# Attention pieces one tile later in the third to seventh chunk, and the second chunk's first weight splits behind an ELU operation

## The chip, the cores and the metric

The kernel runs on one core of a Trainium2 chip. The metric is device time in microseconds (us); the median of three runs of the kernel before is 904.67 us (904.6 to 905.83).

Five engines work side by side, each through its own queue in order: TensorE (PE; its weight loads are listed as PEld), VectorE (DVE), ScalarE (ACT), GpSimd (POOL) and SyncE (SP), which here only issues DMAs. They wait for each other by semaphores.

## What is computed

Attention over 8 batches of 8 heads, 576 positions of 64, then a feed-forward layer on its output, taken as 4608 tokens of 512:

```python
scores = q @ k.T / sqrt(64)           # heads 0-3: a window of 32; heads 4-7: every 4th position of 128
attn = softmax(where(mask, scores, -1e9))
x = (attn @ v).transpose(0, 2, 1, 3).reshape(4608, 512)
h = x @ w_in                          # 512 -> 2048
g = where(h > 0, h, exp(min(h, 0)) - 1)   # ELU
out = g @ w_out                       # 2048 -> 512
```

## The kernel before

**The feed-forward layer** goes by 9 chunks of 512 tokens (`c`, 0 to 8; NCH) and in each by 16 tiles of the 2048 hidden columns (`f`, 0 to 15; NF). For each tile `gemm1` multiplies the chunk's x by a tile of w_in into one PSUM bank `h`; `elu` (L386) makes g of it; `gemm2` (L409) multiplies g by a tile of w_out and adds it into four banks `o_ps`. From chunk 1 on every operand is split into a rounded part and the rest (`xh`, `xl` by `split_x`, L353; `gh`, `gl` by `elu`; the weights `wh`, `wl` by `split_w`, L132), and each product is three products, so that 12 matmuls of 128x512 make a `gemm1` and 12 a `gemm2`. `flush(LAG)` (L491) runs `gemm2` two tiles late: on TensorE the order is product of tile f, output group of tile f-2, product of f+1, output group of f-1. The last output group of a chunk therefore comes in tile 1 of the next one, and with it `store` (L417): four ACT copies `o<-o_ps` (L420), each with its DMA to `out`, through three buffers `o`.

**The ELU operation** is, in chunks 1 to 6: ACT copies h out of its bank (L390), ACT's exponential (L392), DVE's min and add (L401), DVE's max and add (L402), ACT's cast `gh` (L405), DVE's rest `gl` (L406). In those chunks there is a single bank for h, so the next product waits until L390 has copied it. In chunk 0 the banks alternate, ACT runs L392 and L394, and a DVE operation reads the bank and frees it (L397 up to tile 13, L399 for tiles 14 and 15); `hidden` lists these DVE operations, and `hidden[-3]` is that of tile 13.

**The attention** of batch c+1 is made in pieces between the tiles of chunk c. For chunks 1 to 6 the tuple `when` (L508) says behind which tiles they stand: first a scores piece for two head pairs, then their outputs piece, then the same for the other two. A *scores piece* (`scores_piece`, L311) is 144 small matmuls into three banks; after a third of them comes an ACT copy of a single column, `nothing` (L326), which orders the writes into the third bank, and the last third waits for it. DVE adds masks (L279), takes the maxima (L281), subtracts (L288), ACT exponentiates (L289), DVE sums, normalises (L290, L206 to L208) and transposes (L304), once for each head pair; SP loads the next q and k. An *outputs piece* (L336) is 48 matmuls, four ACT copies into `x32` (L194, L197), and loads of v.

**Order.** TensorE's instructions keep the order in which the program is written. On DVE and ACT a scheduler interleaves; `tc.issue_after(ins)` makes the instructions of its block that run on the engine of `ins` come behind it. In chunk 1 the loop at L521 splits the weights that chunk 0 left whole: for each pair an ACT cast and a DVE subtraction (L136, L137). The first two (`split < 2`) come behind the last transposes of batch 1 (`last_transpose[1]`), the others behind `split_x(1)`. A split takes the room of weights split before it, so that ACT's cast waits for an earlier DVE subtraction.

```python
when = () if c == 0 or c >= B - 1 else (0, 6, 7, 13) if c == 1 else (1, 6, 7, 12)
...
while c == 1 and split < min(NF, f + 2):
    left = [t for t in range(2) if wh[need[2 * split + t]] is None]

    with tc.issue_after(last_transpose[1] if split < 2 else last_x):
        if left:
            split_w(split, left[0], left[-1] + 1)
    split += 1
```

Of the kernel before, what the change touches and what calls it, by code (L numbers as in the profile page):

```python
# [18 lines left out]
B, H, S, D = 8, 8, 576, 64  # L19
# [27 lines left out]
def body(ctx: ExitStack, tc: tile.TileContext, q, k, v, masks, w_in, w_out, out):  # L47
# [37 lines left out]
    def load_w(k, behind=None):  # L85

        raw[k] = wst.tile([P, 2, DM], I64, name=f"r{k % NR}")
        if behind is not None:
            nc.gpsimd.tensor_copy(out=raw[k].bitcast(F32)[:QB, :, 0:1], in_=behind[:, 0:2].unsqueeze(2))
        for t in range(2):  # L90
            i = need[2 * k + t]
            nc.sync.dma_start(out=raw[k][:, t, :], in_=(w_in, w_out)[i % 2][i // 2])
# [6 lines left out]
    def magnitude(k):  # L99
        pair = full2[k] = wst.tile([P, 2, DM], F32, name=f"a{k}")  # L100
        for t in range(2):
            full[need[2 * k + t]] = pair[:, t, :]
        return nc.scalar.activation(out=pair.rearrange("p t c -> p (t c)"), in_=halves(k)[1].bitcast(F32), func=AF.Abs)

    def convert(k, keep=lambda ins: ins, part=slice(0, 2 * DM)):

        lo, hi = [u[:, part] for u in halves(k)]
        a = full2[k].rearrange("p t c -> p (t c)")[:, part]
        au = a.bitcast(U32)

        keep(nc.vector.tensor_scalar(out=a, in0=a, scalar1=TINY, scalar2=None, op0=ALU.max))  # L111

        keep(nc.vector.tensor_scalar(out=au, in0=au, scalar1=0x07FFFFFF, scalar2=3, op0=ALU.bitwise_and, op1=ALU.logical_shift_left))  # L113
        keep(nc.vector.scalar_tensor_tensor(out=au, in0=hi, scalar=0xC0000000, in1=au, op0=ALU.bitwise_and, op1=ALU.bitwise_or))  # L114

        return keep(nc.vector.scalar_tensor_tensor(out=au, in0=lo, scalar=29, in1=au, op0=ALU.logical_shift_right, op1=ALU.bitwise_or))  # L116
# [15 lines left out]
    def split_w(k, t0, t1):  # L132

        h, l = space(t1 - t0), space(t1 - t0)
        w = full2[k][:, t0:t1, :]
        nc.scalar.copy(out=h, in_=w)  # L136
        nc.vector.tensor_tensor(out=l, in0=w, in1=h.bitcast(F32), op=ALU.subtract)  # L137
        for t in range(t0, t1):
            wh[need[2 * k + t]], wl[need[2 * k + t]] = h[:, t - t0, :], l[:, t - t0, :]
        if all(wh[need[2 * k + t]] is not None for t in range(2)):  # L140
            spaces.append([f"a{k}", 2])
# [3 lines left out]
    last_transpose = [None] * B  # L145
# [190 lines left out]
    def outputs_piece(made):  # L336

        s = three()
        places = ((s[0], 0, 5), (s[1], 5, 6)), ((s[1][:, QB:], 0, 4), (s[2], 4, 6))
        for place, (b, hp, tr) in zip(places, made):  # L340
            products(place, v_of.pop(b * NPAIR + hp), tr)
        for place, (b, hp, _) in zip(places, made):
            if hp == 0:
                x32[b] = xp.tile([P, NPAIR, S], F32, name="x32", bufs=2)
            copies(b, hp, place)
        for b, hp, _ in made:
            load_v(b * NPAIR + hp + 2)
# [3 lines left out]
    hidden, below = [], []  # L351

    def split_x(c):  # L353
        for hp in range(NC):
            xh[hp] = xp.tile([P, TC], F32R, name=f"xh{hp}")
            xl[hp] = xp.tile([P, TC], F32R, name=f"xl{hp}")
            t0 = c * TC
            while t0 < (c + 1) * TC:
                b, o = divmod(t0, S)
                n = min(S - o, (c + 1) * TC - t0)  # L360
                u = slice(t0 - c * TC, t0 - c * TC + n)
                src = x32[b][:, hp, o:o + n]
                nc.scalar.copy(out=xh[hp][:, u], in_=src)
                last = nc.vector.tensor_tensor(out=xl[hp][:, u], in0=src, in1=xh[hp][:, u].bitcast(F32), op=ALU.subtract)
                t0 += n
        return last.ins
# [14 lines left out]
    def gemm1(c, f):  # L381
        for h_ps in first if (c, f) == (0, 0) else product1(c, f):
            pass
        return h_ps

    def elu(h_ps, c, f):  # L386
        e = fp.tile([P, TC], F32, name="e", bufs=3)
        if 0 < c < B - 1:
            h = fp.tile([P, TC], F32, name="h", bufs=2)
            nc.scalar.copy(out=h, in_=h_ps)  # L390
            h_ps = h
        nc.scalar.activation(out=e, in_=h_ps, func=AF.Exp)  # L392
        if c == 0:
            below.append(nc.scalar.activation(out=e, in_=e, func=AF.Relu, scale=-1.0, bias=1.0).ins)  # L394
            if f < F2:
                g = fp.tile([P, TC], F32, name="gh", bufs=3)
                hidden.append(nc.vector.scalar_tensor_tensor(out=g, in0=h_ps, scalar=0.0, in1=e, op0=ALU.max, op1=ALU.subtract).ins)  # L397
                return g, None
            hidden.append(nc.vector.scalar_tensor_tensor(out=e, in0=h_ps, scalar=0.0, in1=e, op0=ALU.max, op1=ALU.subtract).ins)  # L399
        else:  # L400
            nc.vector.tensor_scalar(out=e, in0=e, scalar1=1.0, scalar2=-1.0, op0=ALU.min, op1=ALU.add)  # L401
            nc.vector.scalar_tensor_tensor(out=e, in0=h_ps, scalar=0.0, in1=e, op0=ALU.max, op1=ALU.add)  # L402
        gh = fp.tile([P, TC], F32R, name="gh", bufs=3)
        gl = fp.tile([P, TC], F32R, name="gl", bufs=2)
        nc.scalar.copy(out=gh, in_=e)  # L405
        nc.vector.tensor_tensor(out=gl, in0=e, in1=gh.bitcast(F32), op=ALU.subtract)  # L406
        return gh, gl
# [79 lines left out]
    split = 0  # L487
# [3 lines left out]
    def flush(n):  # L491
        while len(pend) > n:
            c, f, g = pend.pop(0)
            if f == 0:
                o_of[c] = [ps_o.tile([P, DM], F32, name="o_ps") for _ in range(TC // P)]
            gemm2(o_of[c], g, f)
            if f == NF - 1:
                store(c, o_of.pop(c))

    att = second_attention()  # L500
    for c in range(NCH):
        if c == 1:
            with tc.issue_after(hidden[-4]), tc.issue_after(below[-4]):
                last_x = split_x(c)
        elif c > 1:
            split_x(c)

        when = () if c == 0 or c >= B - 1 else (0, 6, 7, 13) if c == 1 else (1, 6, 7, 12)  # L508
        for f in range(NF):
            while c == 0 and ready < min(NF, f + AHEAD):  # L510
                with tc.issue_after(below[-1] if below else last_copy.ins):
                    magnitude(ready)
                with tc.issue_after(last_conversion.ins):
                    last_conversion = convert(ready)
                if ready + NR < NF:
                    load_w(ready + NR)
                ready += 1
            if c == 0 and f == F1 - 3:
                with tc.issue_after(hidden[-1]), tc.issue_after(below[-1]):
                    split_x(0)  # L520
            while c == 1 and split < min(NF, f + 2):  # L521
                left = [t for t in range(2) if wh[need[2 * split + t]] is None]

                with tc.issue_after(last_transpose[1] if split < 2 else last_x):
                    if left:
                        split_w(split, left[0], left[-1] + 1)
                split += 1
            pend.append((c, f, elu(gemm1(c, f), c, f)))
            if c == 0 and F1 <= f + 2 <= NF:

                with tc.issue_after(hidden[-2]):
                    split_w(f + 1, 0, 2 if f >= F2 else 1)
            if c == 0:
                with tc.issue_after(hidden[-1] if f > 1 else last_step[NPAIR - 1]):
                    next(att)
            flush(LAG)
            if f in when:
                i = when.index(f)
                if i % 2 == 0:
                    made = scores_piece(c + 1, (i, i + 1))  # L540
                else:
                    outputs_piece(made)
# [60 lines left out]
```

## Time and profile before

| | us |
|---|---|
| median of three runs | 904.67 |
| the profiled execution | 905.6 |
| its span, first to last instruction | 903.7 |
| TensorE busy in the span | 883.6 |
| VectorE busy | 581.0 |
| ScalarE busy | 376.7 |

A row of the timeline holds the start in us from the span's start, the duration, engine, line and operation, the tiles (out<-in) and shapes, how many instructions are merged in it, and in brackets how long the engine sat idle before it and what ended that. A row of the windows view holds a stretch, its length, then the busy time of PE, PEld, DVE, ACT and POOL with the number of instructions, the granted TensorE clock, the DMA engines' share and GB/s. A row of the waits holds who waited for whom: us in total, times, longest. Nearly all matmuls have line 83, that of a helper; the tiles' names tell them apart.

### The profile page before, as it was taken

What the parts mean: (1) busy time and instruction counts of PE and PEld (TensorE: products, weight loads), DVE (VectorE), ACT (ScalarE), POOL (GpSimd) and SP (SyncE); (2) the same over time, 40 slices, a digit from 0 to 9 for tenths busy, and PEclk for the clock granted to TensorE, in tenths of its full rate; (3) what the DMA queues carried; (4) which work ended last, traced back from release to release, by engine and by line L of the source; (5) the groups of instructions that cost most, each with busy time, mean ns of one, the idle gap of its engine ahead of it and who ended that gap; (6) DMA issues with size and microseconds to landing.
All of it is one profiled execution on the core that took longest, in us unless ns stands there. A gap on an engine that the chain in (4) does not pass through costs nothing.

```text
span 903.7 us, 15468 instructions
## 1 busy us (share of the span) xinstructions
PE 883.6 (98%) x6540; PEld 695.3 (77%) x6540; DVE 581.0 (64%) x999; ACT 376.7 (42%) x750; POOL 6.0 (1%) x12
## 2 busy tenths in 40 slices
PE   6899999999999999999999999999999999999998
PEld 4544657788878887888788878888788888888886
DVE  5899999966485847694687559574859433343332
ACT  3755767434533343434443343434434432233222
POOL 2000000000000000000000000000000000000000
PEclk8999999999999999999999999999999999999999
DMA  9964103020122013111202111210210010001001
GB/s 341 406 228 145 45 19 100 19 90 1 43 94 89 2 36 102 36 55 36 102 7 84 36 48 54 90 34 2 102 37 1 1 47 1 1 0 47 1 1 46
DMA packets 23796, 59.35 MB, mean 66 GB/s; under 512 B 2640, under 2 KB 2736, under 8 KB 23728
## 3 DMA queue, kind: packets, MB, share of 16 engines
q1 hardware_dynamic: 23728, 58.37, 18.9%
q8 instruction: 51, 0.84, 0.4%
q14 instruction: 17, 0.14, 0.0%
HBM read 48.92 MB, written 9.44 MB: 65 GB/s over the span
## 4 chain that ended last, share of the span: by engine, by line
PE 82%; DVE 8%; DMA 5%; issue 2%; ACT 2%; SPq 0%; ACTq 0%; DVEq 0%
PE h L83 41%; PE o_ps L83 38%; PE a_ps L83 3%; DMA r<-w_out 2%; DVE a L116 1%; DVE a L114 1%; DMA out<-o 1%; DVE a L111 1%; DVE pt L304 1%; DMA r<-w_in 1%; DVE gh L397 1%; DVE r L137 1%; ACT o L420 1%; DVE a L113 1%; DMA kt<-k 1%
## 5 line engine op out<-in xcount | busy, mean ns | idle before, releaser
L83 PE MATMUL o_ps<-a,gh 128*128 128x512 f32 x816 | 267.8, 418 | 0.0
L83 PE MATMUL h<-xh,r 128*128 128x512 f32 x792 | 266.2, 394 | 0.5 <-DVE gh L397 0.5
L83 PEld LDWEIGHTS o_ps<-a,gh 128*128 128x128 f32 x816 | 152.8, 188 | 50.4 <-issue 22.0
L401 DVE TENSOR_SCALAR e<-e 128x512 f32<-128x512 f32 x128 | 54.6, 426 | 191.8 <-ACT e L392 189.9
L83 PEld LDWEIGHTS h<-xh,r 128*128 128x128 f32 x792 | 148.6, 188 | 35.6 <-DVE gh L397 2.1
L83 PE MATMUL h<-xl,r 128*128 128x512 f32 x412 | 160.6, 390 | 0.0
L405 ACT CAST gh<-e 128x512 fp32r<-128x512 f32 x130 | 80.9, 622 | 177.0 <-DVE e L402 176.7
L83 PE MATMUL o_ps<-a,gl 128*128 128x512 f32 x352 | 136.9, 389 | 0.0
L406 DVE TENSOR_TENSOR gl<-e,gh 128x512 fp32r<-128x512 f32 x130 | 89.6, 689 | 71.9 <-ACT gh L405 41.5
L392 ACT ACTIVATE e<-h 128x512 f32<-128x512 f32 x144 | 89.4, 621 | 103.6 <-PE h L83 100.9
L390 ACT COPY h<-h 128x512 f32<-128x512 f32 x96 | 56.2, 585 | 117.7 <-PE h L83 117.6
L304 DVE STREAM_TRANSPOSE pt<-sm 32x384 f32<-32x384 f32 x168 | 95.4, 568 | 2.2
L83 PE MATMUL o_ps<-r,gh 128*128 128x512 f32 x304 | 96.2, 389 | 0.0
L402 DVE SCALAR_TENSOR_TENSOR e<-h,e 128x512 f32<-128x512 f32 x128 | 88.2, 689 | 3.5
L83 PEld LDWEIGHTS h<-xl,r 128*128 128x128 f32 x412 | 77.3, 188 | 17.0 <-issue 1.2
L83 PE MATMUL h<-xh,a 128*128 128x512 f32 x256 | 85.5, 395 | 0.0
L83 PEld LDWEIGHTS o_ps<-a,gl 128*128 128x128 f32 x352 | 66.1, 188 | 13.8
L83 PEld LDWEIGHTS o_ps<-r,gh 128*128 128x128 f32 x304 | 57.1, 188 | 11.8
L83 PE MATMUL o_ps<-r,gl 128*128 128x512 f32 x168 | 65.5, 390 | 0.3 <-DVE gl L406 0.3
L83 PEld LDWEIGHTS h<-xh,a 128*128 128x128 f32 x256 | 48.0, 188 | 11.0
L83 PE MATMUL h<-xl,a 128*128 128x512 f32 x128 | 50.0, 391 | 0.0
L289 ACT ACTIVATE sm<-sm 96x768 f32<-96x768 f32 x24 | 20.4, 849 | 45.0 <-DVE sm L288 45.0
(100 smaller groups left out, 751.4 us busy)
## 6 DMA issues: line engine op xcount, KB each, us to landing
vt<-v SPq DMA_DIRECT2D x30, 384.0 KB, 3.6
kt<-k SPq DMA_DIRECT2D x30, 304.0 KB, 4.6
qt<-q SPq DMA_DIRECT2D x30, 288.0 KB, 3.8
r<-w_in SPq DMA_DIRECT2D x16, 512.0 KB, 8.0
r<-w_out SPq DMA_DIRECT2D x16, 512.0 KB, 8.2
out<-o SPq DMA_DIRECT2D x32, 256.0 KB, 2.8
out<-xl SPq DMA_DIRECT2D x4, 256.0 KB, 2.1
r<-v SPq DMA_DIRECT2D x2, 384.0 KB, 8.3
```

The lines of the kernel that those rows point to most:

```text
L83: return inorder(nc.tensor.matmul(*args, **kw))
L111: keep(nc.vector.tensor_scalar(out=a, in0=a, scalar1=TINY, scalar2=None, op0=ALU.max))
L113: keep(nc.vector.tensor_scalar(out=au, in0=au, scalar1=0x07FFFFFF, scalar2=3, op0=ALU.bitwise_and, op1=ALU.logical_shift_left))
L114: keep(nc.vector.scalar_tensor_tensor(out=au, in0=hi, scalar=0xC0000000, in1=au, op0=ALU.bitwise_and, op1=ALU.bitwise_or))
L289: nc.scalar.activation(out=sm, in_=sm, func=AF.Exp, scale=0.125)
L304: last_transpose[b] = nc.vector.transpose(out=tr[ks, :, cs], in_=sm[cs, :, rs]).ins
L390: nc.scalar.copy(out=h, in_=h_ps)
L392: nc.scalar.activation(out=e, in_=h_ps, func=AF.Exp)
L401: nc.vector.tensor_scalar(out=e, in0=e, scalar1=1.0, scalar2=-1.0, op0=ALU.min, op1=ALU.add)
L402: nc.vector.scalar_tensor_tensor(out=e, in0=h_ps, scalar=0.0, in1=e, op0=ALU.max, op1=ALU.add)
L405: nc.scalar.copy(out=gh, in_=e)
L406: nc.vector.tensor_tensor(out=gl, in0=e, in1=gh.bitcast(F32), op=ALU.subtract)
```

## The change

Two lines change:

```diff
-        when = () if c == 0 or c >= B - 1 else (0, 6, 7, 13) if c == 1 else (1, 6, 7, 12)
+        when = () if c == 0 or c >= B - 1 else (0, 6, 7, 13) if c == 1 else (2, 7, 8, 13)
...
-                with tc.issue_after(last_transpose[1] if split < 2 else last_x):
+                with tc.issue_after(last_transpose[1] if split < 2 else last_x), tc.issue_after(hidden[-3]):
```

In chunks 2 to 6 the four pieces stand behind tiles 2, 7, 8 and 13 in place of 1, 6, 7 and 12. In chunk 1 the weight splits must also stand behind the DVE operation (L397) of chunk 0's tile 13.

The first lines on ACT, at tile 1 of chunk 2, before (h_2363 is the scores piece's third bank, h_2483 the bank of tile 2's product):

```order
L420 COPY o<-o_ps 128x512 x3
L405 CAST gh<-e 128x512
L420 COPY o<-o_ps 128x512
L326 COPY nothing<-h_2363 96x1
L289 ACTIVATE sm<-sm 96x768
L390 COPY h<-h_2483 128x512
L392 ACTIVATE e<-h 128x512
L405 CAST gh<-e 128x512
```

And now (h_2361 is the bank of tile 2's product, h_2402 the piece's third bank):

```order
L420 COPY o<-o_ps 128x512 x3
L405 CAST gh<-e 128x512
L420 COPY o<-o_ps 128x512
L390 COPY h<-h_2361 128x512
L392 ACTIVATE e<-h 128x512
L405 CAST gh<-e 128x512
L326 COPY nothing<-h_2402 96x1
L289 ACTIVATE sm<-sm 96x768
```

The copy `nothing` and the exponential L289 moved from behind the last output copy to behind the ELU operation of tile 2. The same holds in chunks 3 to 6. On DVE the piece's first mask addition (L279) now follows the gl (L406) of tile 2 where it followed that of tile 1.

On DVE at the end of chunk 0 (r_1223, r_1315 and r_1318 are rests of split weights, h_1177 is the bank of tile 13, h_1202 that of tile 14):

```order
 L304 STREAM_TRANSPOSE pt_79<-sm 32x12x32 x6
+L397 SCALAR_TENSOR_TENSOR gh<-h_1177,e 128x512
+L137 TENSOR_TENSOR r_1223<-a_1132,r_1195 128x1024
 L137 TENSOR_TENSOR r_1315<-a_326,r_1223 128x1024
 L137 TENSOR_TENSOR r_1318<-a_474,r_1315 128x1024
-L397 SCALAR_TENSOR_TENSOR gh<-h_1177,e 128x512
-L137 TENSOR_TENSOR r_1223<-a_1132,r_1195 128x1024
 L399 SCALAR_TENSOR_TENSOR e<-h_1202,e 128x512
```

L397 of tile 13 and the split r_1223 moved ahead of the two splits r_1315 and r_1318; the four stand between the same neighbours as before.

On ACT at the same place (the a tiles are weights cast into the room of others, x_539 is batch 1's attention output):

```order
 L392 ACTIVATE e<-h_1202 128x512
+L136 CAST a_1570<-a_540 128x1024
 L194 COPY x_539<-a_ps_1226 128x288
 L394 ACTIVATE e<-e 128x512
+L194 COPY x_539<-a_ps_1227 128x288
 L136 CAST a_1609<-a_616 128x1024
-L194 COPY x_539<-a_ps_1227 128x288
-L136 CAST a_1570<-a_540 128x1024
 L405 CAST gh<-e 128x512
```

The cast a_1570, which takes the room of the weights that r_1223 reads, now stands ahead of tile 14's L394 and of the two copies. The order of SP's DMAs and of POOL's instructions is the same.

## The prediction

> **What bounds the kernel now.** Chunks are counted from 0 (c), their tiles from 0 (f); "the change's chunks" are c = 2 to 6. I read the page's table of busy times first, then two stretches of the windows view.
>
> ```profile
> span 903.7 us, 15468 instructions
> ...
> PE 883.6 (98%) x6540; PEld 695.3 (77%) x6540; DVE 581.0 (64%) x999; ACT 376.7 (42%) x750; POOL 6.0 (1%) x12
> ```
> ```profile
> 225.00:250.00 25.00, 24.30 (x224) 19.98 (x218) 10.90 (x22) 12.95 (x28) 0.00 (x0) 1.00 0.18 61
> 725.00:750.00 25.00, 25.00 (x112) 20.70 (x111) 7.97 (x14) 7.65 (x13) 0.00 (x0) 1.00 0.12 43
> ```
> TensorE is the bound: from 725 to 750, where no piece of attention runs, it is busy all 25.00 us at a granted clock of 1.00 while VectorE (DVE) and ScalarE (ACT) are busy under a third of the time. So the span shrinks only by time in which TensorE waits. From 225 to 250, inside the change's chunks, 0.70 us of it are missing. The view of waits says for what:
>
> ```profile
> PEld h L83 <- ACT nothing L326: 5.4, 5, 1.1
> ...
> PE h L83 <- ACT nothing L326: 4.6, 5, 0.9
> ```
> Five times, once for each of the change's chunks, TensorE waits for the tiny copy `nothing` in the middle of a scores piece. The timeline shows the piece behind tile 1 of chunk 2 (first three rows: its first matmul, the wait, the next tile's first matmul) and the piece behind tile 7 of the same chunk (first matmul, next tile's first matmul):
>
> ```profile
> 248.08 0.24 PE L83 MATMUL h<-kt,qt 64*32 64x64 f32 x1
> ...
> 250.23 0.24 PE L83 MATMUL h<-kt,qt 64*32 64x64 f32 x1 [0.93 <-ACT nothing L326]
> ...
> 250.87 0.50 PE L83 MATMUL h<-xh,r 128*128 128x512 f32 x1
> ...
> 286.13 0.24 PE L83 MATMUL h<-kt,qt 64*32 64x64 f32 x1
> ...
> 287.75 0.50 PE L83 MATMUL h<-xh,a 128*128 128x512 f32 x1
> ```
> The same 144 matmuls take 250.87 - 248.08 = 2.79 us behind tile 1 and 287.75 - 286.13 = 1.62 us behind tile 7. ACT's timeline gives the cause, first around tile 1, then around tile 7:
>
> ```profile
> 246.63 1.54 ACT L420 COPY o<-o_ps 128x512 f32<-128x512 f32 x3
> 248.05 0.64 ACT L405 CAST gh<-e 128x512 fp32r<-128x512 f32 x1
> 249.54 0.59 ACT L420 COPY o<-o_ps 128x512 f32<-128x512 f32 x1 [0.85 <-DMA out<-o]
> 250.02 0.16 ACT L326 COPY nothing<-h 96x1 f32<-96x1 f32 x1
> ...
> 285.99 0.62 ACT L405 CAST gh<-e 128x512 fp32r<-128x512 f32 x1 [1.22 <-DVE e L402]
> 286.87 0.16 ACT L326 COPY nothing<-h 96x1 f32<-96x1 f32 x1 [0.26 <-PE h L83]
> 290.40 0.85 ACT L289 ACTIVATE sm<-sm 96x768 f32<-96x768 f32 x1 [3.37 <-DVE sm L288]
> 291.15 0.57 ACT L390 COPY h<-h 128x512 f32<-128x512 f32 x1
> ```
> Tile 1 is where the previous chunk's four output copies stand. The fourth waits 0.85 us for the DMA that frees its buffer, and `nothing` stands behind it, so it starts 1.94 us into the piece. Behind tile 7 it starts 0.74 us in, after 0.26 us of waiting for TensorE itself, and TensorE does not wait.
>
> **Part one: the pieces of chunks 2 to 6 go one tile later.** Nothing is added or removed: the same 20 pieces (4 in each of 5 chunks) between tiles of the same kind, and the same order on the DMA queue. I go through each.
>
> *First scores piece, tile 1 to 2.* Behind the output copies now come tile 2's h copy, exponential and gh cast, and only then `nothing`: the same row order as at tile 7. I take tile 7's price, 1.62 us, for all five: 5 x (2.79 - 1.62) = 5.85 us gained. The lower bound of this gain by a row is the bare idle time, 4.6 us; the rest, 0.24 us a time, is matmuls that start slowly after the wait, and it goes with the wait.
>
> The Trainium skill, page "Perfetto Trace Analysis", section "Identifying the Most-Contended Engine", holds that matmul busy time misleads on TensorE and that the busy share of weight loads is the measure. By it the gain would be the weight loads' wait in the row above, 5.4 us; the trace here lies past both, since it times the whole piece.
>
> *What the wait covered.* With the piece gone from there, tile 2's product comes straight after the output group and the first tile of the new output group writes the banks that the four copies empty. Chunk 7 has no pieces and is that case already. Its fourth copy, and TensorE's next output group:
>
> ```profile
> 732.13 0.59 ACT L420 COPY o<-o_ps 128x512 f32<-128x512 f32 x1 [0.49 <-DMA out<-o]
> ...
> 733.93 0.39 PE L83 MATMUL o_ps<-r,gh 128*128 128x512 f32 x1
> ```
> The copy is done at 732.72, 1.21 us before the group begins, and the 725 to 750 window has no idle time. In chunk 2 the copy ends at 249.54 + 0.59 = 250.13. How long an output group (and a product) takes is in the chain of waits, and when tile 8's gl is made, behind the piece at tile 7, on VectorE's timeline:
>
> ```profile
> 253.92 2.72 PE o_ps L83 x12
> ```
> ```profile
> 294.35 0.68 DVE L406 TENSOR_TENSOR gl<-e,gh 128x512 fp32r<-128x512 f32 x1
> ```
> Tile 2's product would start where the piece does now, at 248.08, and the group 2.72 later, at 250.80: 0.67 us to spare, and the bank in question is the group's last. I cost it at nothing; were that slack gone, each microsecond would be paid in full. The scheduler also moves VectorE's rows; in chunk 2 alone the piece's six transposes now stand between two ELU operations of tile 3. At tile 7 the next tile's gl is done 295.03 - 286.13 = 8.9 us after the piece starts; 3.48 us of transposes (row further down) make it 12.4, and it is asked for after the piece and five groups, 1.62 + 5 x 2.72 = 15.2. No cost.
>
> *Outputs pieces, 6 to 7 and 12 to 13, and second scores piece, 7 to 8.* Each stays five tiles behind its scores. Chunk 1 has its last outputs piece behind tile 13 before the change. Its last copy:
>
> ```profile
> 226.39 0.34 ACT L194 COPY x<-h 128x192 f32<-128x192 f32 x1
> ```
> All that follows, the split for chunk 2 too, lies in the 225 to 250 window, whose missing 0.70 us are the stall's own (250.23 - 0.93 = 249.30, to 250). So tile 13 costs nothing. The loads that SyncE issues after each piece start a tile later and have five tiles left.
>
> **Part two: weight splits behind the ELU operation of tile 13.** Chunk 0's end, in TensorE's rows (an output group, the wait behind it, a later group of the same kind and its end), VectorE's and ACT's:
>
> ```profile
> 128.88 3.70 PE L83 MATMUL o_ps<-a,gh 128*128 128x512 f32 x8
> 133.08 0.50 PE L83 MATMUL h<-xh,r 128*128 128x512 f32 x1 [0.50 <-DVE gh L397]
> ...
> 137.21 3.70 PE L83 MATMUL o_ps<-a,gh 128*128 128x512 f32 x8
> 140.34 0.79 PE L83 MATMUL h<-xh,r 128*128 128x512 f32 x1
> ```
> ```profile
> 126.57 3.48 DVE L304 STREAM_TRANSPOSE pt<-sm 32x384 f32<-32x384 f32 x6
> 130.06 2.36 DVE L137 TENSOR_TENSOR r<-a,r 128x1024 fp32r<-128x1024 f32 x2
> 132.34 0.69 DVE L397 SCALAR_TENSOR_TENSOR gh<-h,e 128x512 f32<-128x512 f32 x1
> 132.94 1.22 DVE L137 TENSOR_TENSOR r<-a,r 128x1024 fp32r<-128x1024 f32 x1
> 134.07 0.69 DVE L399 SCALAR_TENSOR_TENSOR e<-h,e 128x512 f32<-128x512 f32 x1
> ```
> ```profile
> 134.19 1.05 ACT L136 CAST a<-a 128x1024 fp32r<-128x1024 f32 x1 [0.39 <-DVE r L137]
> 135.15 0.62 ACT L405 CAST gh<-e 128x512 fp32r<-128x512 f32 x1
> ```
> The two splits of 2.36 us stood ahead of L397, which frees a bank of h. It moves from 132.34 to 130.06, when TensorE needs no bank yet, and the wait goes: the group takes 4.20 us (133.08 - 128.88) where its like takes 3.13, so TensorE is 1.07 us early at 133. But VectorE has the same four operations to do: L399 still starts at 134.07, and the cast of 134.19 is only exchanged for another that waits for a split ending at the same time. So gh is cast at 135.15 as before. From there the second chunk's start is paced by VectorE:
>
> ```profile
> 140.00:168.00 28.00, 28.00 (x257) 22.09 (x255) 27.80 (x46) 16.24 (x28) 0.00 (x0) 1.00 0.24 82
> ```
> ```profile
> 167.56 0.69 DVE L406 TENSOR_TENSOR gl<-e,gh 128x512 fp32r<-128x512 f32 x1
> ```
> ```profile
> 168.30 0.50 PE L83 MATMUL o_ps<-r,gl 128*128 128x512 f32 x1 [0.30 <-DVE gl L406]
> ```
> It is busy 27.80 of 28.00 us, and at 168.30 TensorE waits for its gl. That moment doesn't come earlier, so the 1.07 us are spent waiting before it. I take 0. Ends: 1.07 us gained if VectorE could be early after all; 1.05 us lost if the cast that now stands ahead of tile 14's L394 on ACT (its like is the 1.05 us row) holds L399 up by its whole length.
>
> **Sum.** Profiled execution: span 903.7 - 5.85 = 897.9; with the 1.9 us outside its span (905.6 - 903.7) 899.7. Its time lies 0.9 above the runs' median, so against the median: 904.67 - 5.85 = 898.8 us.
>
> **Rivals.**
> *A, both parts pay.* VectorE's run up to 168 has a gap that the early bank fills: 904.67 - 5.85 - 1.07 = 897.8. For: the wait at 133 is real. Against: 27.80 of 28.00. Chance 0.10.
> *B, part of the stall comes back.* `nothing` now stands behind tile 2's gh, which hangs on VectorE. At tile 7 the cast ends at 286.61, 0.26 us before TensorE's results are there, and TensorE wants the bank some 0.2 us after the copy (estimate: two thirds of 1.62 after 286.13 is 287.21, the copy ends 287.03). If gh is 0.5 to 1 us later than that at tile 2, each stall keeps 0.3 to 0.8 us, with the slow restart: 1.5 to 4 us of the gain go, 900.3 to 902.8. Against: before tile 2's ELU VectorE has only ELU work, as before tile 7. Chance 0.10.
> *C, nothing changes.* The wait only changes its name, because `nothing` still stands behind something 1.9 us late: 904.7. The fourth output copy would have to end some 2 us later than 250.13: 0.67 us to tile 2's h copy, the 0.4 us of B, and the 0.93 us of the wait. Chance 0.04.
> *D, slower.* Behind `nothing` on ACT stands the piece's exponential (L289), which holds the next tile's h copy (L390) while it waits for VectorE, and the next product needs that one bank. At tile 7 the copy ends at 291.72; the next product but one starts here:
>
> ```profile
> 293.34 0.39 PE L83 MATMUL h<-xh,r 128*128 128x512 f32 x1
> ```
> So there are 1.6 us to spare, and beyond that TensorE stops. If the six transposes of another piece (3.48 us) came to lie ahead of the subtraction that L289 waits for, each piece would lose 3.48 - 1.6 + 0.24 = 2.1 us, five times 10.6, less 5.85: 909.4. It decides from 1.6 + 0.93 = 2.5 us of delay. Against: the order has the masks' additions right behind tile 2's gl, with no transposes between. Chance 0.04.
>
> **Numbers.** The forecast has 0.72, A 0.10, B 0.10, C 0.04, D 0.04. About 0.2%, 1.8 us, is what a measurement of this kernel can tell from no change, so faster means under 902.9: forecast, A and B, 0.92; same is C, 0.04; slower is D, 0.04. The range runs from A with a little scatter (runs of before lie between 904.6 and 905.83) to the nearer part of B and part two's loss with scatter: 897.3 to 901.2.
>
> **What would show it.** In the profile of the changed kernel: the waits for `nothing` gone from TensorE's list; the scores piece behind tile 2 taking 1.62 us; chunk 2 starting (its first product) at the same time as before within 0.3 us; L397 of tile 13 starting near 130.1, no wait at 133, but a wait for `nothing` or gl between 145 and 168 in its place. Wrong would be: a new wait of TensorE for h copies or output banks at tiles 2 to 4 of chunks 2 to 6, or a chunk 2 that starts 0.5 us or more earlier or later.

## The result, and the profile after

The changed kernel takes 899.28 us (median of 4 runs, 898.99 to 900.04) beside 904.86 us for the kernel before (4 runs, 904.6 to 905.83): a ratio of 0.9937, 95% interval 0.9921 to 0.9952. That is 5.58 us less; 898.8 us was forecast. The profiled execution took 900.04 us with a span of 898.2 us, 5.5 us less than the span before.

In the profile excerpts below, rows between those shown are left out. The page's first table in the changed kernel, then ScalarE's (ACT) waits for the output DMAs and both ways of waiting around `nothing`, two rows of the kernel before and three of the changed one:

```profile
span 898.2 us, 15468 instructions
PE 882.7 (98%) x6540; PEld 695.4 (77%) x6540; DVE 581.0 (65%) x999; ACT 376.3 (42%) x750; POOL 6.0 (1%) x12
```
```profile
ACT o L420 <- DMA out<-o: 5.2, 7, 0.9
ACT nothing L326 <- PE h L83: 1.8, 7, 0.3
```
```profile
ACT o L420 <- DMA out<-o: 4.2, 7, 0.7
ACT nothing L326 <- PE h L83: 2.9, 11, 0.3
PE h L83 <- ACT nothing L326: 0.2, 1, 0.2
```

Before, TensorE waited five times for `nothing` and ACT seven times the other way; now ACT's copy is the one that waits, 11 times of 12. The output copies still wait for their DMA seven times, 4.2 us in all in place of 5.2: most of that wait is still there, but in chunks 2 to 6 TensorE no longer waits for anything behind it. The scores piece behind tile 2 of chunk 2, in the rows that answer to those around tile 1 before (ACT's queue, then TensorE's first matmul of the piece, of its last third and of the next tile):

```profile
249.63 0.59 ACT L420 COPY o<-o_ps 128x512 f32<-128x512 f32 x1 [0.65 <-DMA out<-o]
253.67 0.62 ACT L405 CAST gh<-e 128x512 fp32r<-128x512 f32 x1 [1.22 <-DVE e L402]
254.55 0.15 ACT L326 COPY nothing<-h 96x1 f32<-96x1 f32 x1 [0.26 <-PE h L83]
```
```profile
253.81 0.24 PE L83 MATMUL h<-kt,qt 64*32 64x64 f32 x1
254.78 0.22 PE L83 MATMUL h<-kt,qt 64*32 64x64 f32 x1
255.43 0.50 PE L83 MATMUL h<-xh,r 128*128 128x512 f32 x1
```

`nothing` starts 254.55 - 253.81 = 0.74 us into the piece, after 0.26 us of waiting for TensorE, to the hundredth as behind tile 7 before, and the piece takes 255.43 - 253.81 = 1.62 us. The last third's first matmul starts 0.97 us into the piece and 0.65 us ahead of the product; before, behind the wait, it started 250.23 - 248.08 = 2.15 us in and 250.87 - 250.23 = 0.64 us ahead. So the matmuls behind the wait lost nothing. The 0.24 us by which the stall exceeded its listed 0.93 us lie ahead of the restart: idle time is counted from the end of the last matmul's row, and these rows, 0.22 to 0.24 us long each and 144 of them in 1.62 us, overlap. Two of the stretches in which the kernel before lost time:

```profile
225.00:250.00 25.00, 25.00 (x140) 20.85 (x137) 10.73 (x21) 12.84 (x28) 0.00 (x0) 1.00 0.17 57
250.00:275.00 25.00, 25.00 (x248) 20.61 (x247) 20.23 (x37) 9.18 (x17) 0.00 (x0) 1.00 0.20 67
```

No idle time is left in them. At the seam of chunks 0 and 1, TensorE (the first two matmuls of tile 15's product, the start of chunk 1's scores piece and of its last third, the next product, the output group of tile 2), VectorE (DVE), and the windows view:

```profile
132.26 0.79 PE L83 MATMUL h<-xh,r 128*128 128x512 f32 x1
132.89 0.39 PE L83 MATMUL h<-xl,r 128*128 128x512 f32 x1
145.77 0.24 PE L83 MATMUL h<-kt,qt 64*32 64x64 f32 x1
147.18 0.24 PE L83 MATMUL h<-kt,qt 64*32 64x64 f32 x1 [0.18 <-ACT nothing L326]
147.81 0.50 PE L83 MATMUL h<-xh,r 128*128 128x512 f32 x1
168.54 0.50 PE L83 MATMUL o_ps<-r,gl 128*128 128x512 f32 x1 [0.31 <-DVE gl L406]
```
```profile
126.80 3.48 DVE L304 STREAM_TRANSPOSE pt<-sm 32x384 f32<-32x384 f32 x6
130.31 0.69 DVE L397 SCALAR_TENSOR_TENSOR gh<-h,e 128x512 f32<-128x512 f32 x1
130.91 3.49 DVE L137 TENSOR_TENSOR r<-a,r 128x1024 fp32r<-128x1024 f32 x3
134.32 0.68 DVE L399 SCALAR_TENSOR_TENSOR e<-h,e 128x512 f32<-128x512 f32 x1
```
```profile
140.00:168.00 28.00, 27.79 (x255) 21.82 (x253) 27.80 (x46) 15.91 (x29) 0.00 (x0) 1.00 0.24 82
```

The wait at 133 is gone and tile 15's product starts at 132.26. But this execution runs 0.24 us behind the other by then (transposes at 126.80 against 126.57), and so does L399 (134.32 against 134.07): VectorE's four operations fill the same time in the new order. At 147.18 TensorE now waits for `nothing`, which it did not before, and at 168.54 for gl, again 0.24 us behind. The early bank was given back in between. Four rows of the kernel before (the second matmul of tile 15's product, the start of the piece, the product behind it, tile 3's product), then in the changed kernel the weight loads (PEld) that waited and ScalarE's rows ahead of them:

```profile
133.42 0.40 PE L83 MATMUL h<-xl,r 128*128 128x512 f32 x1
146.32 0.24 PE L83 MATMUL h<-kt,qt 64*32 64x64 f32 x1
147.94 0.50 PE L83 MATMUL h<-xh,r 128*128 128x512 f32 x1
159.09 0.50 PE L83 MATMUL h<-xh,r 128*128 128x512 f32 x1
```
```profile
158.32 0.30 PEld L83 LDWEIGHTS o_ps<-r,gh 128*128 128x128 f32 x2 [0.42 <-ACT o L420]
159.32 0.19 PEld L83 LDWEIGHTS h<-xh,r 128*128 128x128 f32 x1 [0.47 <-ACT h L390]
```
```profile
146.02 1.05 ACT L136 CAST a<-a 128x1024 fp32r<-128x1024 f32 x1 [0.67 <-DVE a L137]
146.98 0.14 ACT L326 COPY nothing<-h 96x1 f32<-96x1 f32 x1
153.42 0.62 ACT L136 CAST a<-a 128x512 fp32r<-128x512 f32 x1 [0.35 <-DVE a L137]
158.68 0.59 ACT L390 COPY h<-h 128x512 f32<-128x512 f32 x1
```

Counted from the output group ahead of tile 15's product (128.88 before, 129.12 after), the piece starts 17.44 us later in the kernel before and 16.65 us later in the changed one: 0.79 us early. It then takes 147.81 - 145.77 = 2.04 us in place of 1.62, which leaves 0.37 us, and tile 3's product starts 30.20 us after the group where it started 30.21: nothing is left. So the early time was gone at 159, ahead of the wait for gl at 168. The first part went to `nothing`, which stood behind a cast that had waited 0.67 us for VectorE: the same kind of stall as behind the output copies. The second went to ScalarE's last output copy and tile 2's h copy, at the end of a stretch in which ScalarE has no gap (153.42 to 159.27) and which begins with another cast that waited for VectorE.

To set this apart from the start, I measure each profile between three matmuls: the output group ahead of chunk 0's tile 15 product, the first product of chunk 2, and the first product of chunk 7. Before, then after:

```profile
128.88 0.70 PE L83 MATMUL o_ps<-a,gh 128*128 128x512 f32 x1
237.11 0.39 PE L83 MATMUL h<-xh,r 128*128 128x512 f32 x1
720.33 0.39 PE L83 MATMUL h<-xh,r 128*128 128x512 f32 x1
```
```profile
129.12 0.70 PE L83 MATMUL o_ps<-a,gh 128*128 128x512 f32 x1
237.40 0.39 PE L83 MATMUL h<-xh,r 128*128 128x512 f32 x1
714.76 0.39 PE L83 MATMUL h<-xh,r 128*128 128x512 f32 x1
```

"Seam" below is the first stretch, 108.23 us before and 108.28 after; "middle" is the second, chunks 2 to 6, 483.22 us before and 477.36 after, 5.86 us less.

### The profile page after: what moved, and what is told of

Read it like the earlier page. It is cut to its first block, busy times and chain, and to the rows that moved or that the text cites. A ratio compares the mean times of both kernels' runs of the same rounds, so it can differ in the third digit from the quotient of the medians.

```text
span 898.2 us, 15468 instructions
## 1 busy us (share of the span) xinstructions
PE 882.7 (98%) x6540; PEld 695.4 (77%) x6540; DVE 581.0 (65%) x999; ACT 376.3 (42%) x750; POOL 6.0 (1%) x12
## 4 chain that ended last, share of the span: by engine, by line
PE 84%; DVE 10%; ACT 2%; issue 2%; DMA 1%; POOL 0%; SPq 0%; DVEq 0%; ACTq 0%
PE h L83 41%; PE o_ps L83 39%; PE a_ps L83 4%; DVE a L116 1%; DVE a L114 1%; DVE r L137 1%; DVE a L111 1%; DVE pt L304 1%; DVE gh L397 1%; DVE a L113 1%; ACT pt L263 1%; DMA kt<-k 1%; DVE sm L208 1%; DMA r<-w_out 0%; ACT sm L269 0%
## 5 line engine op out<-in xcount | busy, mean ns | idle before, releaser
L406 DVE TENSOR_TENSOR gl<-e,gh 128x512 fp32r<-128x512 f32 x130 | 89.5, 689 | 71.8 <-ACT gh L405 42.2
L289 ACT ACTIVATE sm<-sm 96x768 f32<-96x768 f32 x24 | 20.3, 848 | 47.7 <-DVE sm L288 47.7
```

The source lines that it names most:

```text
L289: nc.scalar.activation(out=sm, in_=sm, func=AF.Exp, scale=0.125)
```

## The experiments

The theory is that of the prediction: the gain is five waits for `nothing` behind the output copies, and the early bank is lost to VectorE's backlog. All kernels were timed beside the kernel before; seam and middle are read from the same three matmuls of each profile.

| kernel | us | ratio to before, 95% | seam | middle |
|---|---|---|---|---|
| before | | 1 | 108.23 | 483.22 |
| the change | 899.28 | 0.9937 (0.9921 to 0.9952) | 108.28 | 477.36 |
| pieces alone | 899.33 | 0.9938 (0.9925 to 0.995) | 108.19 | 477.36 |
| splits alone | 905.17 | 1.0 (0.9991 to 1.0009) | 108.23 | 483.29 |
| first piece alone | 899.75 | 0.9943 (0.993 to 0.9955) | 108.24 | 477.39 |
| fourth output elsewhere | 900.2 | 0.9946 (0.9933 to 0.996) | 108.26 | 478.50 |
| one tile earlier | 899.27 | 0.9937 (0.9924 to 0.995) | 108.20 | 477.37 |
| chunk 1 later | 898.01 | 0.9926 (0.9912 to 0.994) | 107.36 | 477.30 |
| chunk 1 later, with the splits | 897.44 | 0.9918 (0.9905 to 0.9931) | 106.57 | 477.29 |

The kernel before took 905.04 us beside the first four experiments and 904.8 beside the last three.

**The two parts, each alone.**

```diff
-        when = () if c == 0 or c >= B - 1 else (0, 6, 7, 13) if c == 1 else (1, 6, 7, 12)
+        when = () if c == 0 or c >= B - 1 else (0, 6, 7, 13) if c == 1 else (2, 7, 8, 13)
```

> Part one alone: the four pieces of chunks 2 to 6 behind tiles 2, 7, 8, 13; the weight splits of chunk 1 as before. Theory (the whole gain is the five waits for `nothing` behind the output copies, 5 x 1.17 us): 5.6 to 5.9 us under the kernel before, as the full change; the stretch from the output group ahead of chunk 0's tile 15 product to chunk 2's first product takes 108.2 us as before. Rival (the splits give about 1 us and the pieces only the bare idle time): 4.6 us under, the stretch unchanged.

```diff
-                with tc.issue_after(last_transpose[1] if split < 2 else last_x):
+                with tc.issue_after(last_transpose[1] if split < 2 else last_x), tc.issue_after(hidden[-3]):
```

> Part two alone: L397 of tile 13 ahead of two weight splits, pieces as before. Theory (VectorE paces TensorE until gl at 168, so the early bank is lost again): within 0.3 us of the kernel before; the wait of 0.5 us at 133 gone, a wait for `nothing` of some 0.2 us near 147 in its place, the stretch from the output group ahead of chunk 0's tile 15 product to chunk 2's first product 108.2 us as before. Rival (the early bank pays): 1.07 us under, the stretch 107.2 us.

The pieces alone were 5.7 us faster (899.33 against 905.04), the splits alone came out the same. With the splits alone TensorE's wait for `nothing` happens six times, the sixth being the new one in chunk 1:

```profile
PE h L83 <- ACT nothing L326: 4.9, 6, 1.0
```

and its tile 15 product starts 131.46 - 128.33 = 3.13 us after the group in place of 4.20, while the seam is what it was:

```profile
128.33 0.70 PE L83 MATMUL o_ps<-a,gh 128*128 128x512 f32 x1
131.46 0.79 PE L83 MATMUL h<-xh,r 128*128 128x512 f32 x1
236.56 0.39 PE L83 MATMUL h<-xh,r 128*128 128x512 f32 x1
```

Both rivals fall: the pieces give 5.86 us in the middle, more than the idle time of 4.6, and the splits give nothing.

**The first piece alone.**

```diff
-        when = () if c == 0 or c >= B - 1 else (0, 6, 7, 13) if c == 1 else (1, 6, 7, 12)
+        when = () if c == 0 or c >= B - 1 else (0, 6, 7, 13) if c == 1 else (2, 6, 7, 12)
```

> Only the first scores piece of chunks 2 to 6 moves, to tile 2; the others stay behind 6, 7 and 12. Theory: all five waits for `nothing` go, 5.85 us; the outputs piece then starts 1.62 + 4 x 5.44 + 0.09 = 23.5 us after its scores piece and wants the second pair's transposes at half of it, 24.6, and they are done at some 24.5 (end of the transposes at tile 1 before, less the 1.17 us of the wait): 5.3 to 5.9 us under the kernel before. Rival (the moves of the other pieces carry part of the gain): under 4.7 us.

5.3 us faster by the medians, and the middle shrinks by 5.83 us: the moves of the other three pieces carry nothing, and the 0.4 us between its median and that of the pieces alone does not lie there. What the other moves give, by this working, is room. With four tiles between scores and outputs the last transposes (VectorE) and the outputs piece (TensorE) stand like this in chunk 2:

```profile
274.06 3.48 DVE L304 STREAM_TRANSPOSE pt<-sm 32x384 f32<-32x384 f32 x6
```
```profile
276.86 1.87 PE L83 MATMUL a_ps<-pt,vt 128*64 128x96 f32 x40
```

The transposes end at 277.54. The piece lasts until the next product at 278.99, 2.13 us, and the second pair's products begin at half of it (an estimate), at 277.9: some 0.4 us to spare.

**The fourth output copy without its DMA wait.** The pieces stay behind tile 1.

```diff
-            o = fp.tile([P, DM], F32, name="o", bufs=3) if c < NCH - 1 else xp.tile([P, DM], F32, name=f"xl{t}")
+            o = (fp.tile([P, DM], F32, name="h", bufs=2) if t == TC // P - 1 and c < B - 2 else
+                 fp.tile([P, DM], F32, name="o", bufs=3) if c < NCH - 1 else xp.tile([P, DM], F32, name=f"xl{t}"))
```

> Pieces and splits as before; the fourth output copy of each chunk writes to one of the two buffers of ELU's h instead of a third-generation output buffer, so that it waits for no output DMA. Theory (`nothing` is late because of what stands ahead of it in ScalarE's queue): the fourth copy starts at the cast's end, about 0.85 us earlier, `nothing` likewise, and TensorE's wait falls from 0.93 to 0.1 to 0.2 us with or without its slow restart of 0.24: 3.5 to 4.5 us under the kernel before. Rival (the place in the program, not the queue, makes the piece slow): no change.

```profile
247.68 0.64 ACT L405 CAST gh<-e 128x512 fp32r<-128x512 f32 x1
248.20 0.61 ACT L421 COPY h<-o_ps 128x512 f32<-128x512 f32 x1
248.68 0.17 ACT L326 COPY nothing<-h 96x1 f32<-96x1 f32 x1
```
```profile
247.72 0.24 PE L83 MATMUL h<-kt,qt 64*32 64x64 f32 x1
249.54 0.50 PE L83 MATMUL h<-xh,r 128*128 128x512 f32 x1
```

The copy follows the cast at once, `nothing` starts 0.96 us into the piece in place of 1.94, and the piece takes 1.82 us in place of 2.79. The medians differ by 4.8 us, the middle by 4.72: above the 3.5 to 4.5 that were expected, since only 0.2 us a piece remain. No idle time of TensorE is listed for them: the last third starts at 248.91, while the row of the matmul ahead of it lasts to 248.94. So the piece was slow because of what stood ahead of `nothing` in ScalarE's queue, and most of that was one wait for a DMA.

**One tile earlier in place of later.**

```diff
-        when = () if c == 0 or c >= B - 1 else (0, 6, 7, 13) if c == 1 else (1, 6, 7, 12)
+        when = () if c == 0 or c >= B - 1 else (0, 6, 7, 13) if c == 1 else (0, 5, 6, 11)
```

> The pieces of chunks 2 to 6 go one tile the other way, behind tiles 0, 5, 6 and 11; splits as before. Theory (only tile 1 is bad, because the output copies stand there): the scores piece takes 1.62 us and the gain is that of the change, 5.85 us; up to 0.5 us a chunk less if the piece's exponential and the output copies now hold back an h copy on ScalarE. Rival (later is better, since it leaves VectorE and ScalarE more time after the chunk's start): no gain, or slower than before.

The gain is the same, 5.85 us in the middle. So later is not better as such: of tiles 0, 1 and 2 only tile 1 is bad. And a wait is free as long as TensorE needs nothing behind it in time: here the output copies wait far longer for their DMA than in any other kernel.

```profile
ACT o L420 <- DMA out<-o: 10.1, 7, 2.2
```

**The seam.** Two kernels move chunk 1's pieces as well, which takes the first scores piece's VectorE work out of the backlog; the first keeps the splits as before, the second is the full change.

```diff
-        when = () if c == 0 or c >= B - 1 else (0, 6, 7, 13) if c == 1 else (1, 6, 7, 12)
+        when = () if c == 0 or c >= B - 1 else (3, 8, 9, 14) if c == 1 else (2, 7, 8, 13)
```

> Part one, and chunk 1's pieces behind tiles 3, 8, 9, 14 instead of 0, 6, 7, 13; splits as before. It takes the first scores piece's VectorE work out of the stretch in which VectorE has no gap. Theory (VectorE's backlog paces chunk 1's start): the waits at 159 and at 168 (about 0.9 us over the plain pace together) go, the wait at 133 stays: the stretch from the output group ahead of chunk 0's tile 15 product to chunk 2's first product falls from 108.2 to some 107.4 us, 6.6 us under the kernel before. Rival (ScalarE's casts and output copies pace it): stretch as before, 5.8 us under.

> The full change, and chunk 1's pieces behind tiles 3, 8, 9, 14. Theory (part two gave nothing because VectorE's backlog took it back): with the backlog thinned the early bank pays, 0.7 to 1.1 us beyond the same kernel without part two: stretch from the output group ahead of chunk 0's tile 15 product to chunk 2's first product some 106.5 us, about 7.5 us under the kernel before. Rival (the early bank never pays, whatever paces the stretch): the same as without part two.

VectorE's part (the third busy time) of the stretch, without and with the splits' move:

```profile
140.00:168.00 28.00, 28.00 (x261) 23.08 (x260) 22.66 (x32) 16.93 (x29) 0.00 (x0) 1.00 0.21 68
```
```profile
140.00:168.00 28.00, 28.00 (x260) 23.07 (x260) 23.48 (x35) 16.96 (x30) 0.00 (x0) 1.00 0.24 75
```

VectorE is busy 22.66 and 23.48 of 28 us where it was busy 27.80, TensorE all of it. Without the splits' move the seam falls by 0.87 us to 107.36, with it by another 0.79 to 106.57. So the early bank pays once the scores piece is out of the stretch. That the thinner VectorE is the reason is argued and not shown: the two kernels move the piece's work on TensorE, ScalarE and VectorE at once, with `nothing` and the output copies' place among it, and those copies are where the early time had gone. The bank pays 0.79 us and not 1.07, because the 1.07 went by the start of the product's first matmul, and that row is itself longer without a wait. TensorE in the kernel without the splits' move, the product and the small matmuls of attention behind it:

```profile
132.25 0.50 PE L83 MATMUL h<-xh,r 128*128 128x512 f32 x1 [0.50 <-DVE gh L397]
135.24 0.96 PE L83 MATMUL a_ps<-pt,vt 128*64 128x96 f32 x18
```

and with it:

```profile
131.44 0.79 PE L83 MATMUL h<-xh,r 128*128 128x512 f32 x1
134.69 1.21 PE L83 MATMUL a_ps<-pt,vt 128*64 128x96 f32 x24
```

From start to start the product takes 2.99 us behind a wait and 3.25 without one; with the group ahead of it (from 128.05 and 128.30) it is 7.19 and 6.39, a difference of 0.80. The kernel with both is the fastest here, 897.44 us, below the change: its 7.4 us under the kernel before are 5.93 in the middle and 1.66 in the seam, with 0.2 lost elsewhere or to scatter.

## Why the prediction was right

- *The bound.* Time was to be had where TensorE waited: the middle shrank by what the five stalls cost from start to start, and TensorE is busy in all of the two stretches shown.
- *First scores piece, 5 x 1.17 = 5.85 us.* The middle fell by 5.86. Pricing the whole piece, and not the idle time beside the wait (4.6) or the weight loads' wait (5.4), was right; the fourth-output experiment shows the difference too: with no idle time listed the piece still takes 0.2 us more than 1.62. One reading in it was wrong and cost nothing: the 0.24 us beside the idle time are no slow matmuls behind the wait (0.64 us to the product behind it, 0.65 without one) but part of the wait.
- *What the wait covered, and the other pieces: nothing.* No new wait of TensorE between chunks 2 and 6; the experiment that moves the first piece alone has the same middle.
- *Part two: 0 in place of 1.07.* Seam 108.28 against 108.23. The result was forecast, the reason in part. The prediction named VectorE's gl at 168 as the moment that would not come earlier; the early time was gone by 159, 0.42 us of it behind `nothing` and 0.37 at ScalarE's output copy and h copy. Ahead of both in ScalarE's queue stand casts that waited for VectorE, so by this trace VectorE holds TensorE back through that queue; how much of the second part is ScalarE's own work is open. The size was off too: by a mark that the wait leaves alone, the second matmul of the product, its price is (133.42 - 128.88) - (132.89 - 129.12) = 0.77 us. It did not enter the sum.
- *The sum, 898.8 us.* Measured 899.28, inside the range. Of the 0.5 us by which it missed, 0.19 are the median of before, which came out at 904.86 in place of 904.67. The other 0.27 are within scatter: the stretch ahead of the seam, which no edit touches, took 128.05 to 129.12 us in the nine profiles.
- *Rivals.* A fell to the splits alone, B to the unchanged 0.74 us of `nothing`, C to the piece's 1.62 us, D to the middle, in which TensorE waits for no h copy.

Not tried: how late tile 2's gh may come before TensorE waits again (rivals B and D), since no run came near it.

## What to carry to other kernels

On an engine whose queue runs in order, ask of each small instruction that the bound engine waits for what stands ahead of it there, DMA waits among it; moving the waiter to another place of the loop, or giving the blocked instruction a free buffer, are two cures for the same wait. Price a stall by the start-to-start time of the whole piece against its undisturbed twin, not by the idle time that the waits list. And before counting a wait that goes, look for the next engine that paces the same stretch: here VectorE was busy 27.80 of 28.00 us behind it and held ScalarE's queue back, and the gain came only when a piece of work was moved out of there.

## What had not been expected of the hardware

What a stall of TensorE costs can't be read at the rows beside it, in either direction. Inside the scores piece the stall cost 1.17 us where 0.93 us idle were listed, and in the fourth-output experiment 0.2 us a piece with none listed, since overlapping rows of 0.22 to 0.24 us hide the wait's beginning. At tile 15's product it is the other way round: the first matmul starts 1.07 us later behind the wait, but the second only 0.77 us. Without the wait the first matmul's row starts at once and is longer (0.79 us against 0.50). Neither a slow restart nor a faster stream behind a stall is needed to explain these times. Why the first row is longer was not tested.
